# A partition of raw keys and values holds two neighbouring tokens, and the gathers and the mask follow

## The chip, the core and the metric

The kernel runs on one core of one Trainium2 chip. The metric is the device time of one execution in microseconds (us), of which several are taken; lower is better. Engines are named as in the profile: PE (TensorE matmuls) and PEld (its weight loads), DVE (VectorE), ACT (ScalarE), POOL (GpSimd) and SP (SyncE, which here only issues DMAs).

## What is computed

Block-sparse attention followed by a two-layer feed-forward network. There are 4 batches, 8 heads, 768 tokens and a head dimension of 64; blocks have 32 tokens, so there are 24 of them.

```python
batch, n_heads, seq, head_dim = (4, 8, 768, 64)
block = 32
rand_blocks = np.random.randint(0, n_blocks, size=(n_blocks, 3))
...
scores = scale * np.matmul(q, k.transpose(0, 1, 3, 2))
mask = np.abs(blk_i - blk_j) <= window
mask = mask | (blk_i == 0) | (blk_j == 0) | (blk_i == n_blocks - 1) | (blk_j == n_blocks - 1)
for qb in range(n_blocks):
    for kb in sampled_blocks[qb]:
        mask[qb * block:(qb + 1) * block, kb * block:(kb + 1) * block] = True
scores = np.where(mask, scores, -1000000000.0)
attn = np.exp(scores - np.max(scores, axis=-1, keepdims=True))
attn = attn / (np.sum(attn, axis=-1, keepdims=True) + 1e-09)
x = np.matmul(attn, v)          # then (B*S, H*D) = (3072, 512)
...
h = x @ w_in                    # 512 x 2048
out = np.maximum(0.01 * h, h) @ w_out
```

A query block sees its neighbours, the first and the last block, and 3 sampled blocks. The first and the last query block see every key.

## The kernel before

**Tiling.** Two query blocks (64 queries) make a tile T; there are 12 in a batch. T = 0 is the first and the last block together, which see all 768 keys. The others see 384 keys (`KEYS`, 12 slots of 32): a window of 128 tokens from (T-1)*64 on, two end blocks in the last two slots, and in slots 4 to 9 the 3 sampled blocks of each of the two query blocks. A unit is one T and one pair of heads (`hp`), a step of the main loop is one unit, and four tiles T make an item, whose feed-forward part follows later. Every number is carried as two fp16 halves, high and low.

**Keys.** `load_k` (L487) loads a head's 768 x 64 fp32 keys with one DMA: token 128*c + p goes to partition p, chunk c, so each DMA has 768 runs of 256 bytes (192 KB). `prep_k` (L496) takes the sum of squares on ACT, scales, splits into halves and sends them through one DMA transpose into `kt` [128, head, token]. `gather_k` (L587) builds `kg` [128, head, 384] for a tile T: one DVE copy for the window (L593, 8 heads x 128 tokens), one for the two end blocks (L596, done once a batch for each of two buffers), and six POOL copies for the sampled blocks (L602), each at a token offset read from `offs`. It ends with `em` (L607), where POOL spreads the mask of the 12 slots over 32 keys each. `em` is added to the scores (L666).

**Values.** `load_v` (L431) loads the same way. `prep_v` (L437) scales, splits, and writes the halves of a head pair to a DRAM tensor `scr` [768 tokens, 8 heads x 128 fp16], 2 KB a token, with one DMA (L464). `gather_v` (L616) fetches the 384 rows of a tile: one straight DMA for the window (L621), one for each end block (L625, once a batch for each of two buffers), and two indirect DMAs from POOL for the sampled rows (L628), whose row numbers `rows` are made in `build_masks`. The first tile T = 0 reads values from `v16s` in SBUF, in the order of the load.

**Masks.** `build_masks` (L225) makes `offs`, `rows` (block number * 32 or'ed with the lane of the partition) and `mask` [128, 11, 12] fp32: zero, or a large negative number where a slot is not to be counted.

**Order.** The main loop writes the order of work by hand, by a string of letters for each step; side work (loads, `prep_k`, `prep_v`, `prep_q`, weights) is spread between steps as generators. K loads of batch 0 come first of all, then constants, Q, V; K of the next batch follows from step 26 on (for batch 0) or 6 on, V of the next batch from step 28 on. All DMAs except the indirect ones are issued by SP in one queue, the loads, the transposes of `kt`, `qs` and `pt` (L704, probabilities), the `vg` gathers and the outputs. In the first 200 us the feed-forward weights are also loaded (64-bit numbers, decoded with integer operations on DVE, L326 to L330) and split into halves.

```python
t = pa.tile([P, 2, NC, D], F32, tag="rk", ...)
nc.sync.dma_start(out=t[:, h], in_=k[b, 2 * hp + h].rearrange("(c p) d -> p c d", p=P))
...
nc.vector.tensor_copy(out=kg[:, :, :P], in_=kt[:, :, t0:t0 + P])
...
nc.sync.dma_start(out=vg[:, 0, :], in_=scr[b][t0:t0 + P, :])
```

Of the kernel before, what the change touches and what calls it, by code (L numbers as in the profile page):

```python
# [12 lines left out]
BF16 = mybir.dt.bfloat16  # L13
F32 = mybir.dt.float32
I32 = mybir.dt.int32
# [4 lines left out]
P = 128  # L20
BLOCK = 32
WINDOW = 1
NEG = -(2.0 ** 120)
# [42 lines left out]
def tile_block_sparse_attention_ffn(  # L66
# [142 lines left out]
    lane = cst.tile([P, 1], I32, name="lane")  # L209
    mask = cst.tile([P, NT - 1, SLOTS], F32, name="mask")  # L210

# [12 lines left out]

    def build_masks():  # L225
        nc.vector.tensor_scalar(
            out=offs, in0=row.rearrange("p (a b) -> p a b", b=2)[:, :, 0], scalar1=5, scalar2=None,
            op0=ALU.logical_shift_left)
        nc.gpsimd.iota(lane, pattern=[[0, 1]], base=0, channel_multiplier=1)
        nc.vector.tensor_scalar(out=lane, in0=lane, scalar1=BLOCK - 1, scalar2=None, op0=ALU.bitwise_and)  # L230
        flat_rows = rows.rearrange("p c t -> p (c t)")
# [21 lines left out]
        for a in range(2):  # L253
# [5 lines left out]
        nc.vector.tensor_scalar(  # L259
            out=mask[:, :, 4:10], in0=pm.rearrange("p t a r -> p t (a r)"), scalar1=-1.0, scalar2=-NEG,  # L260
            op0=ALU.add, op1=ALU.mult)
        nc.vector.memset(mask[:, :, :4], 0.0)
        nc.vector.memset(mask[:, :, 10:], 0.0)
        for hh in range(2):
            a, b = (slice(D * hh + BLOCK * i, D * hh + BLOCK * (i + 1)) for i in range(2))
            nc.vector.memset(mask[a, :, 3:4], NEG)
            nc.vector.memset(mask[b, :, 0:1], NEG)
            nc.vector.memset(mask[a, 0:1, 10:11], NEG)
            nc.vector.memset(mask[b, NT - 2:NT - 1, 11:12], NEG)

# [158 lines left out]
    vscale, vraw, v16s, scr, vg = {}, {}, {}, {}, {}  # L429

    def load_v(b, hp):  # L431
        t = pa.tile([P, NC, 2, D], F32, tag="v", name=f"v_{b}_{hp}", bufs=5)
        for h in range(2):
            nc.sync.dma_start(out=t[:, :, h, :], in_=v[b, 2 * hp + h].rearrange("(c p) d -> p c d", p=P))
        vraw[b, hp] = t

    def prep_v(b):  # L437
# [14 lines left out]
        for hp in range(NP):  # L452
            raw = vraw.pop((b, hp))
# [13 lines left out]
            yield 1.2  # L467
# [19 lines left out]
    def load_k(b, hp):  # L487
        if b == 0:
            t = early_k[:, hp * S:(hp + 1) * S].rearrange("p (h c d) -> p h c d", h=2, c=NC)
        else:  # L490
            t = pa.tile([P, 2, NC, D], F32, tag="rk", name=f"rk_{b}_{hp}", bufs=CFG["rk"])
        for h in range(2):
            nc.sync.dma_start(out=t[:, h], in_=k[b, 2 * hp + h].rearrange("(c p) d -> p c d", p=P))
        return t
# [92 lines left out]
    def gather_k(b, T):  # L587
# [4 lines left out]
        t0 = (T - 1) * Q2  # L592
        nc.vector.tensor_copy(out=kg[:, :, :P], in_=kt[:, :, t0:t0 + P])  # L593
        if ends.get(n) != b:
            ends[n] = b
            nc.vector.tensor_copy(  # L596
                out=kg[:, :, KEYS - Q2:].rearrange("p h (n l) -> p h n l", l=BLOCK),
                in_=kt.rearrange("p h (n l) -> p h n l", l=BLOCK)[:, :, 0:NB:NB - 1, :])
        for slot, i in sampled_of(T):
            begin = len(nc.cur_bb.bb.instructions)  # L600
            off = nc.gpsimd.value_load(offs[:1, i:i + 1], min_val=0, max_val=S - BLOCK)
            nc.gpsimd.tensor_copy(  # L602
                out=kg[:, :, slot * BLOCK:(slot + 1) * BLOCK], in_=kt[:, :, bass.ds(off, BLOCK)])
# [3 lines left out]
        nc.gpsimd.tensor_copy(  # L607
            out=em.rearrange("p (n l) -> p n l", l=BLOCK),
            in_=mask[:, T - 1, :].unsqueeze(2).to_broadcast([P, SLOTS, BLOCK]))
        kgs[b, T] = kg, em  # L610
# [5 lines left out]
    def gather_v(b, T):  # L616
# [3 lines left out]
        t0 = (T - 1) * Q2  # L620
        nc.sync.dma_start(out=vg[:, 0, :], in_=scr[b][t0:t0 + P, :])  # L621
        if vends.get(n) != b:
            vends[n] = b
            for i, at in enumerate((0, S - BLOCK)):
                nc.sync.dma_start(  # L625
                    out=vg[Q2 + i * BLOCK:Q2 + (i + 1) * BLOCK, 2, :], in_=scr[b][at:at + BLOCK, :])
        for c, n_ in ((1, P), (2, Q2)):
# [577 lines left out]
```

## Time and profile before

| what | value |
|---|---|
| median of 3 runs | 893.37 us (889.02 to 898.08) |
| the profiled execution | 889.45 us, its span 887.7 us |
| mean granted TensorE clock | 0.948 |
| DMA packets | 328,450 (139.25 MB), 295,453 of them under 512 bytes |
| DMAs from SP | 322,718 packets, 66.8% of 16 engines' span |
| K loads (8 into W, 24 into rk) | 32, 192 KB each |
| V loads | 32, 192 KB each, 4.5 us to landing |
| straight gathers of V | 44 of 256 KB, 3.9 us to landing; 16 of 64 KB, 5.3 us |

The span is what the profile covers; about 2 us of the execution lie around it. In the profile a line such as "L602 POOL COPY kg<-kt" is an instruction of line 602 that writes kg from kt. SPq is SP's issuing queue: the time in its rows is that of issuing, not of the transfer. In the view of a tile or a line, three numbers divided by strokes are the least, the median and the longest duration in ns. The view of waits gives the total in us, how often, and the longest. "W<-in_k_dram" are the K loads of batch 0, which use a part of the weights' tile that is still empty.

### The profile page before, as it was taken

To read this page: it belongs to the slowest core of one execution; us is meant where nothing else is said; L and a number is where in the kernel's file an instruction comes from. 1 tells how busy PE (TensorE), PEld (TensorE's weight loads), DVE (VectorE), ACT (ScalarE), POOL (GpSimd) and SP (SyncE) were. 2 spreads that over 40 slices of the span, in tenths; PEclk is the share of its full clock that TensorE was granted. 3 is DMA by queue.
4 is the path that set the end of the run, shared out by engine and by line. 5 is a ranking of instruction groups with operands and counts; after the bars stand their busy time and mean duration, and the time that the engine had idled before them with its cause. 6 is when DMAs were issued, how large, how long until landed. Compare 5 with 4: busy or idle time off the path is not lost. (4 is left out here: it accounts for less than half of the span.)

```text
span 887.7 us, 19902 instructions
## 1 busy us (share of the span) xinstructions
PE 739.8 (83%) x7020; PEld 488.9 (55%) x7020; DVE 624.9 (70%) x1623; ACT 485.8 (55%) x1063; POOL 432.7 (49%) x558
## 2 busy tenths in 40 slices
PE   0234655877999998888999999999899999999997
PEld 0213433645666665555656565656556666656674
DVE  2799898997977886773857867789657677754121
ACT  3666768665655764562645846556536454543211
POOL 0046767565236465664343475476325565633221
PEclk9999555989999999999999999999999999999999
DMA  6998999967679989893558979768836596654000
GB/s 138 272 298 192 280 208 234 207 146 170 141 165 182 197 156 194 137 212 89 145 97 157 217 145 195 169 136 184 194 59 135 106 183 154 126 100 103 20 7 25
DMA packets 328450, 139.25 MB, mean 157 GB/s; under 512 B 295453, under 2 KB 307742, under 8 KB 328350
## 3 DMA queue, kind: packets, MB, share of 16 engines
q1 hardware_dynamic: 322718, 120.67, 66.8%
q0 software_dynamic: 5632, 17.31, 7.6%
q8 instruction: 55, 0.90, 0.4%
q14 instruction: 45, 0.37, 0.1%
HBM read 65.58 MB, written 12.58 MB: 88 GB/s over the span
## 5 line engine op out<-in xcount | busy, mean ns | idle before, releaser
L792 PE MATMUL o<-W,g 128*128 128x512 f16 x1152 | 276.3, 384 | 7.9 <-DVE g L778 6.0
L765 PE MATMUL h<-x,W 128*128 128x256 f16 x2304 | 275.3, 276 | 2.4 <-DVE wi_tot L140 1.1
L765 PEld LDWEIGHTS <-W 128*128 128x128 f16 x2304 | 224.9, 100 | 51.1 <-issue 12.8
L779 POOL TENSOR_TENSOR g<-ht,g 128x512 f16<-128x512 f32 x96 | 114.8, 1196 | 216.8 <-DVE g L778 169.1
L602 POOL COPY kg<-kt 128x256 f16 x264 | 131.4, 521 | 97.0 <-PE s L659 47.7
L792 PEld LDWEIGHTS <-g 128*128 128x128 f16 x1152 | 107.7, 99 | 128.9 <-issue 14.5
L677 ACT ACTIVATE p<-p,mx 128x384 f32<-128x384 f32 x208 | 125.9, 606 | 93.0 <-DVE mx L666 70.8
L699 DVE SCALAR_TENSOR_TENSOR pp<-p,r,pp 128x384 f16<-128x384 f32 x208 | 147.9, 737 | 40.4 <-ACT pp L695 39.1
L695 ACT ACTIVATE pp<-p,r 128x384 f16<-128x384 f32 x208 | 115.6, 605 | 43.8 <-issue 12.9
L628 POOL DMA_INDIRECT vg<-scr,rows x88 | 95.0, 1080 | 61.0 <-PE av L730 40.9
L774 DVE SCALAR_TENSOR_TENSOR ht<-ht 128x512 f32<-128x512 f32 x96 | 71.1, 741 | 75.3 <-ACT ht L771 74.9
L666 DVE CUSTOM_DVE_ANT_0 p<-s,em,nsc 128x384 f32<-128x384 f32 x176 | 101.9, 611 | 25.5 <-PE s L659 25.2
L730 PE MATMUL av<-pt,vg 128*64 128x128 f16 x2112 | 84.8, 230 | 20.6 <-DMA pt<-pp 15.0
L730 PEld LDWEIGHTS <-vg 128*64 128x64 f16 x2112 | 73.5, 117 | 47.3 <-issue 41.3
L771 ACT ACTIVATE ht<-h,gd 128x512 f32<-128x512 f32 x80 | 54.1, 676 | 78.8 <-PE h L765 43.4
L659 PE MATMUL s<-kg,qs_q 128*64 128x384 f16 x352 | 65.6, 368 | 25.0 <-DVE mx L666 20.2
L659 PEld LDWEIGHTS <-qs_q 128*64 128x64 f16 x416 | 28.4, 116 | 85.1 <-issue 46.1
L659 PE MATMUL s<-kg,qxs_q 128*64 128x384 f16 x352 | 64.3, 360 | 6.3 <-DMA qxs_q<-qs_q 6.3
L778 DVE CAST g<-ht 128x512 f16<-128x512 f32 x96 | 43.9, 457 | 12.4 <-PE o L792 10.3
L748 POOL TENSOR_TENSOR x<-xf,x 128x256 f16<-128x256 f32 x48 | 37.1, 773 | 27.8 <-ACT x L746 27.3
L685 DVE TENSOR_SCALAR sum<-sum 128x2 f32<-128x2 f32 x96 | 30.9, 322 | 22.0 <-ACT p L677 21.3
L534 ACT ACTIVATE qa_q<-rq 128x512 f16<-128x512 f32 x25 | 15.7, 626 | 51.8 <-DMA rq<-in_q_dram 40.3
(129 smaller groups left out, 753.6 us busy)
## 6 DMA issues: line engine op xcount, KB each, us to landing
vg<-scr SPq DMA_DIRECT2D x44, 256.0 KB, 3.9
v<-in_v_dram SPq DMA_DIRECT2D x32, 192.0 KB, 4.5
qxs_q<-qs_q SPq DMA_DIRECT2D x48, 128.0 KB, 3.1
scr<-v SPq DMA_DIRECT2D x16, 384.0 KB, 4.2
W<-in_moe_w_in_dram SPq DMA_DIRECT2D x5, 1024.0 KB, 5.9
rq<-in_q_dram SPq DMA_DIRECT2D x20, 256.0 KB, 5.3
out_dram<-ob SPq DMA_DIRECT2D x20, 256.0 KB, 3.4
rk<-in_k_dram SPq DMA_DIRECT2D x24, 192.0 KB, 4.8
```

Source lines behind the costliest of these rows:

```text
L602: nc.gpsimd.tensor_copy(out=kg[:, :, slot * BLOCK:(slot + 1) * BLOCK], in_=kt[:, :, bass.ds(off, BLOCK)])
L628: nc.gpsimd.indirect_dma_start(out=vg[:n_, c, :], out_offset=None, in_=scr[b][:, :], in_offset=bass.IndirectOffsetOnAxis(ap=rows[:n_, c - ...
L659: nc.tensor.matmul(o, a, k, start=(n == 0), stop=(n == 1)))
L666: nc.vector.tensor_tensor_reduce(out=u.p[i], in0=u.sp[i], in1=kgs[u.b, u.T][1] if u.T else zero.to_broadcast([P, KEYS]), scale=u.nsc, scal ...
L677: nc.scalar.activation(u.p[i], u.p[i], AF.Exp, scale=-1.0, bias=u.mx[:, :1], accum_out=u.pair.sum[:, u.pi, i:i + 1])
L695: nc.scalar.activation(pp[:, 0, :], p, AF.Copy, scale=u.r)
L699: nc.vector.scalar_tensor_tensor(out=pp[:, 1, :], in0=p, scalar=u.r, in1=pp[:, 0, :], op0=ALU.mult, op1=ALU.subtract)
L730: nc.tensor.matmul(o, a, m, start=(c == 0 and l == 0), stop=(c == n - 1 and l == 1)))
L765: nc.tensor.matmul(c.ph[:, i], w, x, start=(d == 0 and m == 0), stop=(d == NP - 1 and m == 2)))
L774: nc.vector.scalar_tensor_tensor(out=c.t, in0=c.t, scalar=0.01, in1=c.t, op0=ALU.mult, op1=ALU.max)
L779: nc.gpsimd.tensor_tensor(out=c.g[:, 1], in0=c.t, in1=c.g[:, 0], op=ALU.subtract)
L792: nc.tensor.matmul(o, a, w, start=(c.first and i == 0 and m == 0), stop=(c.last and i == 1 and m == 2)))
```

## The change

K and V are loaded so that partition p of chunk c holds tokens 256*c + 2*p and 256*c + 2*p + 1, which are adjacent in DRAM. A load then has 384 runs of 512 bytes. In the chunks of 128 the even tokens of 256 come first and the odd ones after, and what follows is brought into that order:

- `kt` keeps its shape; its columns are even tokens, then odd tokens, by 256.
- Each run of tokens in `kg` and `vg` is in that order too: 64 even and 64 odd ones in the window, 16 and 16 in each end block and sampled block. The window copy has 2 x 64 elements for each head and is cut in two where the window crosses from one 256-token chunk into the next; the end blocks are two copies; a sampled block is copied as 2 x 16 elements.
- `scr` still has one row a token, in the order of tokens; each head pair is written by two DMAs, one for the even and one for the odd rows. The straight gathers of V are two DMAs each, every second row.
- `offs` and the lanes of `rows` are worked out for that order, with a few more integer operations.
- `mask` has two entries for each slot (even, odd) in bf16, and `em` spreads each over 16 keys. The window's masked blocks are then columns 3 and 7, or 0 and 4.

```diff
-    mask = cst.tile([P, NT - 1, SLOTS], F32, name="mask")
+    mask = cst.tile([P, NT - 1, 2 * SLOTS], BF16, name="mask")
...
+        at_row = row.rearrange("p (a b) -> p a b", b=2)
         nc.vector.tensor_scalar(
-            out=offs, in0=row.rearrange("p (a b) -> p a b", b=2)[:, :, 0], scalar1=5, scalar2=None,
-            op0=ALU.logical_shift_left)
+            out=offs, in0=at_row[:, :, 0], scalar1=3, scalar2=8,
+            op0=ALU.logical_shift_right, op1=ALU.logical_shift_left)
+        nc.vector.tensor_scalar(
+            out=at_row[:, :, 1], in0=at_row[:, :, 0], scalar1=7, scalar2=4,
+            op0=ALU.bitwise_and, op1=ALU.logical_shift_left)
+        nc.vector.tensor_tensor(out=offs, in0=offs, in1=at_row[:, :, 1], op=ALU.bitwise_or)
...
-        nc.vector.tensor_scalar(out=lane, in0=lane, scalar1=BLOCK - 1, scalar2=None, op0=ALU.bitwise_and)
+        nc.vector.tensor_scalar(
+            out=odd, in0=lane, scalar1=4, scalar2=1, op0=ALU.logical_shift_right, op1=ALU.bitwise_and)
+        nc.vector.tensor_scalar(
+            out=lane, in0=lane, scalar1=HB - 1, scalar2=1, op0=ALU.bitwise_and, op1=ALU.logical_shift_left)
+        nc.vector.tensor_tensor(out=lane, in0=lane, in1=odd, op=ALU.bitwise_or)
...
+    pairs = lambda t: t.rearrange("p (c r) d -> p c (r d)", r=2)
...
-        t = pa.tile([P, NC, 2, D], F32, tag="v", name=f"v_{b}_{hp}", bufs=5)
+        t = pa.tile([P, 2, NC, D], F32, tag="v", name=f"v_{b}_{hp}", bufs=5)
         for h in range(2):
-            nc.sync.dma_start(out=t[:, :, h, :], in_=v[b, 2 * hp + h].rearrange("(c p) d -> p c d", p=P))
+            nc.sync.dma_start(out=pairs(t[:, h]), in_=v[b, 2 * hp + h].rearrange("(c p r) d -> p c (r d)", p=P, r=2))
...
-            nc.sync.dma_start(
-                out=scr[b].rearrange("(c p) (g x) -> p g c x", p=P, g=NP)[:, hp],
-                in_=v16.rearrange("p c x d -> p c (x d)"))
+            for r in range(2):
+                nc.sync.dma_start(
+                    out=scr[b].rearrange("(c p r) (g x) -> p r g c x", p=P, r=2, g=NP)[:, r, hp],
+                    in_=v16[:, r::2].rearrange("p c x d -> p c (x d)"))
...
-            nc.sync.dma_start(out=t[:, h], in_=k[b, 2 * hp + h].rearrange("(c p) d -> p c d", p=P))
+            nc.sync.dma_start(out=pairs(t[:, h]), in_=k[b, 2 * hp + h].rearrange("(c p r) d -> p c (r d)", p=P, r=2))
...
-        nc.vector.tensor_copy(out=kg[:, :, :P], in_=kt[:, :, t0:t0 + P])
+        ktv = kt.rearrange("p h (c r t) -> p h c r t", r=2, t=P)
+        win = kg[:, :, :P].rearrange("p h (r j) -> p h r j", r=2)
+        c0, a0 = t0 // (2 * P), t0 % (2 * P) // 2
+        n0 = min(Q2, P - a0)
+        nc.vector.tensor_copy(out=win[:, :, :, :n0], in_=ktv[:, :, c0, :, a0:a0 + n0])
+        if n0 < Q2:
+            nc.vector.tensor_copy(out=win[:, :, :, n0:], in_=ktv[:, :, c0 + 1, :, :Q2 - n0])
...
-            nc.vector.tensor_copy(
-                out=kg[:, :, KEYS - Q2:].rearrange("p h (n l) -> p h n l", l=BLOCK),
-                in_=kt.rearrange("p h (n l) -> p h n l", l=BLOCK)[:, :, 0:NB:NB - 1, :])
+            for i, (c, at) in enumerate(((0, 0), (NC // 2 - 1, P - HB))):
+                nc.vector.tensor_copy(
+                    out=kg[:, :, KEYS - Q2 + i * BLOCK:KEYS - Q2 + (i + 1) * BLOCK].rearrange(
+                        "p h (r j) -> p h r j", r=2),
+                    in_=ktv[:, :, c, :, at:at + HB])
...
+            first = kt[:, :, bass.ds(off, HB)]
+            src = bass.AP(first.tensor, first.offset, [*first.ap[:-1], [P, 2], first.ap[-1]],
+                          runtime_checks=first.runtime_checks, dep_tracking_offset=first.dep_tracking_offset)
             nc.gpsimd.tensor_copy(
-                out=kg[:, :, slot * BLOCK:(slot + 1) * BLOCK], in_=kt[:, :, bass.ds(off, BLOCK)])
+                out=kg[:, :, slot * BLOCK:(slot + 1) * BLOCK].rearrange("p h (r j) -> p h r j", r=2), in_=src)
...
-            out=em.rearrange("p (n l) -> p n l", l=BLOCK),
-            in_=mask[:, T - 1, :].unsqueeze(2).to_broadcast([P, SLOTS, BLOCK]))
+            out=em.rearrange("p (n l) -> p n l", l=HB),
+            in_=mask[:, T - 1, :].unsqueeze(2).to_broadcast([P, 2 * SLOTS, HB]))
...
-        nc.sync.dma_start(out=vg[:, 0, :], in_=scr[b][t0:t0 + P, :])
+        for r in range(2):
+            nc.sync.dma_start(out=vg[r * Q2:(r + 1) * Q2, 0, :], in_=scr[b][t0 + r:t0 + P:2, :])
...
-                nc.sync.dma_start(
-                    out=vg[Q2 + i * BLOCK:Q2 + (i + 1) * BLOCK, 2, :], in_=scr[b][at:at + BLOCK, :])
+                for r in range(2):
+                    nc.sync.dma_start(
+                        out=vg[Q2 + i * BLOCK + r * HB:Q2 + i * BLOCK + (r + 1) * HB, 2, :],
+                        in_=scr[b][at + r:at + BLOCK:2, :])
```

In the diff `HB` is 16, `P` 128, `Q2` 64, `NC` 6 and `BLOCK` 32.

More of the change, by code (lines that the diff above doesn't have):

```diff
@@ L21 @@
 BLOCK = 32
+HB = BLOCK // 2
 WINDOW = 1
@@ L225, in build_masks @@
     def build_masks():
+        at_row = row.rearrange("p (a b) -> p a b", b=2)
         nc.vector.tensor_scalar(
-            out=offs, in0=row.rearrange("p (a b) -> p a b", b=2)[:, :, 0], scalar1=5, scalar2=None,
-            op0=ALU.logical_shift_left)
-        nc.gpsimd.iota(lane, pattern=[[0, 1]], base=0, channel_multiplier=1)
-        nc.vector.tensor_scalar(out=lane, in0=lane, scalar1=BLOCK - 1, scalar2=None, op0=ALU.bitwise_and)
+            out=offs, in0=at_row[:, :, 0], scalar1=3, scalar2=8,
[4 more added lines that the diff above has]
+        nc.vector.tensor_tensor(out=offs, in0=offs, in1=at_row[:, :, 1], op=ALU.bitwise_or)
+        nc.gpsimd.iota(lane, pattern=[[0, 1]], base=0, channel_multiplier=1)
+        odd = cst.tile([P, 1], I32, name="odd")
+        nc.vector.tensor_scalar(
[3 more added lines that the diff above has]
+        nc.vector.tensor_tensor(out=lane, in0=lane, in1=odd, op=ALU.bitwise_or)
         flat_rows = rows.rearrange("p c t -> p (c t)")
@@ L259, in build_masks @@
         nc.vector.tensor_scalar(
[L260 to L263, printed above, removed]
+            out=mask[:, :, 8:20].rearrange("p t (n i) -> p t n i", i=2),
+            in0=pm.rearrange("p t a r -> p t (a r)").unsqueeze(3).to_broadcast([P, NT - 1, 2 * NR, 2]),
+            scalar1=-1.0, scalar2=-NEG, op0=ALU.add, op1=ALU.mult)
+        nc.vector.memset(mask[:, :, :8], 0.0)
+        nc.vector.memset(mask[:, :, 20:], 0.0)
         for hh in range(2):
             a, b = (slice(D * hh + BLOCK * i, D * hh + BLOCK * (i + 1)) for i in range(2))
[L266 to L269, printed above, removed]
+            nc.vector.memset(mask[a, :, 3:8:4], NEG)
+            nc.vector.memset(mask[b, :, 0:8:4], NEG)
+            nc.vector.memset(mask[a, 0:1, 20:22], NEG)
+            nc.vector.memset(mask[b, NT - 2:NT - 1, 22:], NEG)
     WI = 512
@@ L452, in prep_v @@
         for hp in range(NP):
-            raw = vraw.pop((b, hp))
+            raw = vraw.pop((b, hp)).rearrange("p h c d -> p c h d")
             if hp:
@@ L592, in gather_k @@
         t0 = (T - 1) * Q2
[L593 removed]
+        ktv = kt.rearrange("p h (c r t) -> p h c r t", r=2, t=P)
[5 more added lines that the diff above has]
+            nc.vector.tensor_copy(out=win[:, :, :, n0:], in_=ktv[:, :, c0 + 1, :, :Q2 - n0])
         if ends.get(n) != b:
             ends[n] = b
[L596 to L598 removed]
+            for i, (c, at) in enumerate(((0, 0), (NC // 2 - 1, P - HB))):
[3 more added lines that the diff above has]
+                    in_=ktv[:, :, c, :, at:at + HB])
         for slot, i in sampled_of(T):
             begin = len(nc.cur_bb.bb.instructions)
[L601 removed]
+            off = nc.gpsimd.value_load(offs[:1, i:i + 1], min_val=0, max_val=S - P - HB)
+            first = kt[:, :, bass.ds(off, HB)]
+            src = bass.AP(first.tensor, first.offset, [*first.ap[:-1], [P, 2], first.ap[-1]],
+                          runtime_checks=first.runtime_checks, dep_tracking_offset=first.dep_tracking_offset)
             nc.gpsimd.tensor_copy(
[L603 removed]
+                out=kg[:, :, slot * BLOCK:(slot + 1) * BLOCK].rearrange("p h (r j) -> p h r j", r=2), in_=src)
             in_order("k", begin)
```

## Prediction

> **What bounds the kernel now.** I read the page's table of busy time and its 40 slices first, to see which engine fills which stage.
>
> ```profile
> span 887.7 us, 19902 instructions
> ...
> PE 739.8 (83%) x7020; PEld 488.9 (55%) x7020; DVE 624.9 (70%) x1623; ACT 485.8 (55%) x1063; POOL 432.7 (49%) x558
> ...
> PE   0234655877999998888999999999899999999997
> ...
> DVE  2799898997977886773857867789657677754121
> ```
>
> The reader is to see two stages. Up to about 200 us (nine slices of 22.2 us) PE is half empty and DVE is nearly full; after that PE is full. The view by windows puts numbers on it (its columns are the stretch, its length, busy time of PE, PEld, DVE, ACT, POOL, the granted clock, the DMA share and GB/s).
>
> ```profile
> core 0: us, PE busy (x) PEld busy (x) DVE busy (x) ACT busy (x) POOL busy (x), PEclk, DMA share, GB/s
> 0.00:200.00 200.00, 97.44 (x920) 68.25 (x921) 165.23 (x423) 129.66 (x251) 102.02 (x120) 0.81 0.94 219
> 16.00:22.00 6.00, 0.00 (x0) 0.00 (x0) 0.00 (x0) 0.00 (x0) 0.00 (x0) 1.00 0.17 14
> 30.00:40.00 10.00, 2.90 (x17) 1.91 (x16) 7.27 (x34) 8.71 (x18) 0.00 (x0) 1.00 1.02 308
> 40.00:50.00 10.00, 3.05 (x18) 1.96 (x19) 9.90 (x18) 5.57 (x7) 0.00 (x0) 1.00 1.19 226
> 220.00:887.00 667.00, 626.79 (x5917) 409.45 (x5915) 444.71 (x1155) 345.84 (x792) 320.11 (x427) 0.99 0.69 138
> 5.70:9.50 3.80, 1.17 (x4) 1.00 (x4) 1.05 (x8) 2.90 (x6) 0.00 (x0) 1.00 1.30 227
> 10.00:14.00 4.00, 0.00 (x0) 0.00 (x0) 1.64 (x4) 2.85 (x7) 0.00 (x0) 1.00 1.03 302
> 37.00:41.00 4.00, 1.46 (x10) 1.20 (x10) 2.69 (x8) 3.27 (x5) 0.00 (x0) 1.00 1.03 405
> 430.00:430.60 0.60, 0.60 (x5) 0.29 (x3) 0.57 (x2) 0.60 (x2) 0.00 (x0) 1.00 0.96 292
> ```
>
> From 220 us on PE is busy 626.8 of 667 us: only 40 us are left there. In the first 200 us DVE is busy 165.2 and DMA 0.94 of its time; from 40 us DVE has no gap (9.90 of 10). So what decides the length of the first stage is when DVE's saturated stretch can begin (DMA decides that), and how much work DVE then has. The third view, the timeline of SP's queue, shows what stands ahead of that:
>
> ```profile
> 3.78 4.16 SPq L493 DMA_DIRECT2D W<-in_k_dram  x6
> ...
> 11.24 4.78 SPq L221 DMA_DIRECT2D rows<-in_sampled_blocks_dram  x6
> 16.11 4.36 SPq L523 DMA_TRANSPOSE kt<-W  x1
> ...
> 26.44 5.57 SPq L434 DMA_DIRECT2D v<-in_v_dram  x6
> ...
> 33.90 8.62 SPq L493 DMA_DIRECT2D rk<-in_k_dram  x4
> 42.62 5.87 SPq L523 DMA_TRANSPOSE kt<-W  x3
> ```
>
> K loads fill the DMA engines to 9.5 us, the first weight load follows (302 GB/s to 14 us), and then 16 to 22 us shows only the crawl of the `rows` loads (14 GB/s) with every engine idle: they began when the weights had ended. Everything up to here is a chain of transfers; the next stretch, V loads, three weight loads and four K loads of batch 1, is one too (DMA share 1.02 and 1.19), until kt of head pairs 1 to 3 is transposed.
>
> **The change part by part.**
>
> *Longer runs.* Each of the 32 K and 32 V loads moves 192 KB (196,608 bytes) in 768 runs of 256 bytes; after the change in 384 of 512. The row 5.70:9.50 is K loads almost alone: 227 GB/s, so 0.87 us a load. For 512-byte runs the nearest row is 430.00:430.60, writes of `scr`: 292 GB/s, so 0.67 us. That saves 0.19 us a load, 12.4 us of DMA time in all. The lower end is nothing (a store is not a load); the upper end is the 405 GB/s of the weights' 4 KB runs: 0.49 us, a saving of 0.38. I take 0.19, since that row has the same run length. On the path lie batch 0's eight K loads (8 x 0.19 = 1.5 us, ahead of weights, `rows` and the first transpose) and its eight V loads, ahead of the weights that DVE decodes from 40 us: 1.5 us. The four of batch 1 (0.8 us) hold up the last three transposes, but at that time DVE is full, so they count nothing. Sum: -3.0 us. If DVE's stretch were held by something else, all of it would be hidden.
>
> The remaining 44 loads save 8.4 us of the DMA time after 40 us. After 220 us that engine-time could only shorten the waits of PE on DMA:
>
> ```profile
> PE s L659 <- DVE mx L666: 8.1, 6, 1.9
> PE av L730 <- DMA pt<-pp: 7.5, 4, 2.9
> PE s L659 <- DMA qxs_q<-qs_q: 6.7, 7, 1.7
> PE s L659 <- DMA qs_q<-qa_q: 5.7, 2, 3.2
> ```
>
> Those three DMA waits are 19.9 us together; 8.4 us of 667 x 0.69 = 460 us of DMA time is 1.8%, so -0.4 us.
>
> *More DMAs.* Each straight gather of V becomes two of 64 rows (44 to 88), the end blocks 16 to 32, the writes of `scr` 16 to 32: 76 more issues on SP.
>
> ```profile
> L621 SPq DMA_DIRECT2D vg<-scr x44: 325/408/3042, 75.8 to 808.9; - x44
> ...
> L625 SPq DMA_DIRECT2D vg<-scr x16: 377/415/953, 76.4 to 642.4; - x16
> ```
>
> At the median 0.41 us that is 31 us of SP. The second of each pair waits for nothing new (the first has waited for the same buffer); behind it stand the transposes of `pt`, for which PE waits 4 times after 220 us, and the q transposes. Cover is the lag between a transpose and its use; without it each issue costs up to 0.41 us at a place where PE waits (13 such waits in the rows above: 5.3 us, the upper end; the lower end is zero). I take one in the first stage and one later: +0.8 us.
>
> *DVE.* The window copy keeps its 1,024 elements but is two copies where the window crosses a 256-token chunk (T = 4 and 8, 8 times in all), and the end blocks are two copies instead of one (8 times). The view of the tile kg in the first 200 us (least, median and longest time in ns):
>
> ```profile
> L602 POOL COPY kg<-kt x64: 386/402/1457, 51.1 to 199.9; 128x256 f16 x64
> L593 DVE COPY kg<-kt x11: 400/552/1273, 52.2 to 198.8; 128x1024 f16<-128x1024 f16 x11
> L596 DVE COPY kg<-kt x2: 277/280/283, 52.5 to 53.3; 128x512 f16<-128x512 f16 x2
> ```
>
> L596 already copies in runs of 32 elements, and from 512 to 1,024 elements the least time grows by 123 ns, so the fixed part is about 150 ns: shorter runs cost nothing, each extra copy 0.15 us. Before 200 us that is 4 copies, +0.6 us on a full DVE. The four more integer operations in build_masks fall into DVE's idle 16 to 22 us, the mask twice as wide is one small operation at 28 us, with the POOL copies that need it 20 us later: zero, covered by those gaps, and under 1 us if they close.
>
> *POOL.* The 264 sampled copies keep their 256 elements, in 16 runs of 16 instead of 8 of 32; em keeps 384, in 24 runs of 16 (its source is now bf16).
>
> ```profile
> L607 POOL CAST em<-mask x10: 497/502/1365, 29.0 to 190.1; 128x384 bf16<-128x384 f32 x10
> ```
> ```profile
> L779 POOL TENSOR_TENSOR g<-ht,g x96: 1141/1156/1999, 168.6 to 878.5; 128x512 f16<-128x512 f32 x96
> ```
> ```profile
> L748 POOL TENSOR_TENSOR x<-xf,x x48: 657/672/1380, 102.4 to 840.2; 128x256 f16<-128x256 f32 x48
> ```
> ```profile
> L387 POOL TENSOR_TENSOR W<-W x12: 2114/2135/3111, 61.0 to 173.1; 128x1024 f16<-128x1024 f32 x12
> ```
>
> The first is em in the same 200 us, the others are the lines of three POOL subtractions. From 386 ns (8 runs, 256 elements) and 497 (12 runs, 384) a run of 32 costs 28 ns. If all of that were the run and none the elements, 8 more runs would add 222 ns and 12 more 333: the upper end. The lower end is zero, and the nearest row speaks for it: L748 walks 4 runs of 64, and lies on the line through the unbroken L779 and L387 (1.90 ns an element, 168 fixed: 654 for 256, measured 657). I take zero.
>
> *Sum.* -3.0 - 0.4 + 0.8 + 0.6 = -2.0 us. Against the profiled execution (889.45 us, of which the span is 887.7) that gives 887.5; this execution is 3.9 us below the median of the runs shown, so as a median 893.4 - 2.0 = 891.4 us.
>
> **The rivals.**
>
> *A, the loads gain far more.* If 512-byte runs went at the rate of 4 KB runs (405 GB/s) and every load before 200 us counted (20 to 43 us, and the eight V loads of batch 1, issued from step 28 on), 28 x 0.38 = 10.6 us would go; less 1.0 for the DVE copies and one issue: 883.8 us. For it: DMA share 0.94 over 200 us. Against it: 292 GB/s for 512 bytes, and DVE's 9.90 of 10. The Trainium skill, DMA: Bandwidth & Descriptors, section Specifications, speaks for this case: it puts the least transfer for line rate at 512 bytes. This trace does not agree as far as it shows: 512-byte stores stay at 292 GB/s where 4 KB loads reach 405.
>
> *B, POOL's short runs.* At the upper end the 64 sampled copies and 10 of em before 200 us cost 64 x 0.222 + 10 x 0.333 = 17.5 us, and where DVE is full a copy that DVE then waits for costs one for one: 893.4 - 2.0 + 17.5 = 908.9 us. It eats the gain from 31 ns a copy, and is slower by 1% from 62% of the bound (138 ns a copy). For it: L593 has a least time of 400 ns and a longest of 1,273, so DVE copies do get held up. Against: L748. The Trainium skill, SBUF — State Buffer, section SBUF: two separate sides, says that DVE and GpSimd take a shared pair of ports as an exclusive lock for a whole instruction; the spread of L593 agrees.
>
> *C, the gain is hidden.* DVE's stretch is held by the weights' arrival and its own work, not by K and V: then only the costs stay, +0.6 + 0.4: 894.4 us. For it: DVE is full from 40 us; against: from 16 to 22 us and for 2.7 us between 30 and 40 it stands idle while transfers run.
>
> **How the numbers follow.** The forecast has 0.45, with its own range 889 to 895 (from 3.0 + 0.8 + 0.4 us of gain and no cost, to the costs of 1.4 alone); A 0.20, B 0.15, C 0.20. The range 883 to 902 takes in A, C and 60% of B's bound. A difference under 1% cannot be told from no change here (the three runs lie 1% apart). Faster by over 1% is A: 0.20. Slower by over 1% is B beyond 138 ns, 0.12; the rest, 0.68, is within 1%.
>
> **What would show it.** The window in which the K loads stand alone should reach about 290 GB/s, and the first kt transpose be issued some 1.5 us before 16.11, the three later ones 3 to 4 us before 42.62. L602's least time should stay at 386 ns (from 420 on B is at work) and the copies L593 at 400 for 1,024 elements. PE's busy time after 220 us should not change. The prediction is wrong if kt comes no earlier, if DVE's busy time before 200 us grows by over 2 us, or if SP's extra issues appear as waits of PE on pt.

## The result, and the profile after

| | median | of runs | ratio to before |
|---|---|---|---|
| kernel before | 894.70 us (889.02 to 901.92) | 20 | |
| changed kernel | 900.15 us (895.40 to 907.86) | 20 | 1.0068, 95% interval 1.0043 to 1.0093 |

The change makes the kernel 0.7% (6 us) slower. The forecast was 891.4 us, 2 us faster. The time lies within the range and within 1% of before, but on the other side of no change, and clear of it. The profiled execution took 897.59 us, of which the span is 895.6. Ratios here and below leave out runs that took over 1.5% more than the fastest of the same kernel, and need not be the quotient of the medians beside them.

First the page's busy time, then the view by windows (columns as before: stretch, length, busy time of PE, PEld, DVE, ACT and POOL, granted clock, DMA share, GB/s).

```profile
span 895.6 us, 20016 instructions
...
PE 744.0 (83%) x7020; PEld 487.7 (54%) x7020; DVE 630.3 (70%) x1643; ACT 486.7 (54%) x1063; POOL 425.5 (48%) x558
```
```profile
0.00:200.00 200.00, 95.57 (x896) 63.89 (x897) 166.63 (x419) 127.14 (x245) 92.58 (x115) 0.81 0.90 213
5.20:8.50 3.30, 1.17 (x4) 1.00 (x4) 0.84 (x7) 2.51 (x6) 0.00 (x0) 1.00 0.96 266
16.00:22.00 6.00, 0.00 (x0) 0.00 (x0) 2.49 (x9) 0.00 (x0) 0.00 (x0) 1.00 0.19 12
40.00:50.00 10.00, 3.21 (x20) 1.99 (x18) 9.39 (x29) 5.32 (x10) 5.91 (x12) 1.00 1.01 328
220.00:887.00 667.00, 628.84 (x5919) 410.50 (x5917) 447.57 (x1171) 347.67 (x796) 321.02 (x430) 0.98 0.72 139
```

The engines' work is nearly the same: PE 744 us against 740, DVE 630 against 625, POOL 425 against 433. In the first 200 us, though, PE has done fewer matmuls (896 against 920) with DVE as full as before. The K loads reach 266 GB/s in place of 227, and the crawl from 16 to 22 us is still there. The timeline of SP's queue shows what became of the earlier start:

```profile
3.65 3.27 SPq L508 DMA_DIRECT2D W<-in_k_dram  x6
...
10.35 6.34 SPq L222 DMA_DIRECT2D rows<-in_sampled_blocks_dram  x6
16.79 4.27 SPq L538 DMA_TRANSPOSE kt<-W  x1
...
30.59 8.88 SPq L538 DMA_TRANSPOSE kt<-W  x3
...
53.48 3.66 SPq L508 DMA_DIRECT2D rk<-in_k_dram  x3
```

Two things stand here. The loads ahead of `rows` are issued 0.9 us sooner, but the six `rows` loads now take 6.34 us to issue instead of 4.78, and the first kt transpose comes at 16.79 instead of 16.11. And the queue has another order: the three later kt transposes stand ahead of the K loads of batch 1 (30.59 against 53.48), where before they stood behind them. Nobody wrote that order by hand. The program writes its instructions down in one sequence, and a planner then places them on each engine by times that it estimates itself; it planned the changed program anew.

The view of kg in the first 200 us, and the two straight gathers from the view of vg:

```profile
L628 POOL COPY kg<-kt x60: 386/401/882, 41.9 to 195.0; 128x256 f16 x60
L612 DVE COPY kg<-kt x10: 288/452/642, 42.5 to 191.6; 128x1024 f16<-128x1024 f16 x8, 128x512 f16<-128x512 f16 x2
L618 DVE COPY kg<-kt x4: 213/410/424, 43.0 to 44.6; 128x256 f16<-128x256 f16 x4
```
```profile
L648 SPq DMA_DIRECT2D vg<-scr x88: 444/588/1586, 74.9 to 817.2; - x88
L653 SPq DMA_DIRECT2D vg<-scr x32: 406/418/2159, 76.2 to 650.2; - x32
```

POOL's copies take 386 ns at the least and 401 at the median, as before: short runs cost POOL nothing. But a gather of 64 rows takes 0.588 us to issue, longer than one of 128 rows did (0.408).

### The profile page after: what moved, and what is told of

It reads as the page before. It is cut to its first block, busy times and chain, and to the rows that moved or that the text cites. A ratio compares the mean times of both kernels' runs of the same rounds, so it can differ in the third digit from the quotient of the medians.

```text
span 895.6 us, 20016 instructions
## 1 busy us (share of the span) xinstructions
PE 744.0 (83%) x7020; PEld 487.7 (54%) x7020; DVE 630.3 (70%) x1643; ACT 486.7 (54%) x1063; POOL 425.5 (48%) x558
## 5 line engine op out<-in xcount | busy, mean ns | idle before, releaser
L794 PE MATMUL h<-x,W 128*128 128x256 f16 x2304 | 278.3, 278 | 5.3 <-DVE q_tot L141 2.7
L794 PEld LDWEIGHTS <-W 128*128 128x128 f16 x2304 | 225.5, 100 | 56.5 <-issue 18.2
L728 DVE SCALAR_TENSOR_TENSOR pp<-p,r,pp 128x384 f16<-128x384 f32 x208 | 151.2, 751 | 48.3 <-ACT pp L724 44.4
L628 POOL COPY kg<-kt 128x256 f16 x264 | 124.4, 493 | 82.7 <-PE s L688 37.7
L688 PE MATMUL s<-kg,qs_q 128*64 128x384 f16 x352 | 63.8, 360 | 39.0 <-DVE mx L695 35.3
L759 PEld LDWEIGHTS <-vg 128*64 128x64 f16 x2112 | 71.3, 116 | 41.7 <-issue 35.0
L714 DVE TENSOR_SCALAR sum<-sum 128x2 f32<-128x2 f32 x96 | 37.0, 386 | 19.8 <-ACT p L706 19.2
L777 POOL TENSOR_TENSOR x<-xf,x 128x256 f16<-128x256 f32 x48 | 37.3, 777 | 21.2 <-ACT x L775 20.3
```

The costliest lines, as they stand in the source:

```text
L628: nc.gpsimd.tensor_copy(out=kg[:, :, slot * BLOCK:(slot + 1) * BLOCK].rearrange("p h (r j) -> p h r j", r=2), in_=src)
L688: nc.tensor.matmul(o, a, k, start=(n == 0), stop=(n == 1)))
L728: nc.vector.scalar_tensor_tensor(out=pp[:, 1, :], in0=p, scalar=u.r, in1=pp[:, 0, :], op0=ALU.mult, op1=ALU.subtract)
L759: nc.tensor.matmul(o, a, m, start=(c == 0 and l == 0), stop=(c == n - 1 and l == 1)))
L794: nc.tensor.matmul(c.ph[:, i], w, x, start=(d == 0 and m == 0), stop=(d == NP - 1 and m == 2)))
```

## Experiments

The runs e1 to e4, e5 to e8, e9 to e11, e12 to e14, e15 and e16, e17 and e18 each shared a chip with runs of the kernel before; each ratio is to those runs. The same kernel came out 0.2 to 0.4% apart on two chips (below), so differences within a group weigh most. The quotient of the medians would be up to 0.4% away from the ratio (0.998 for e3, 1.015 for e7): a difference that small is weak evidence by itself.

### Is it the order or the contents?

To part the two, the order in which one kernel's engines run can be written into another. Instructions of the two programs are matched by line and operation; then each is tied to the one ahead of it on its engine, without a wait, so that the planner has no choice left (`ORDER` holds one list for each engine). Additional instructions stand right behind their partners. Tying them costs nothing that shows: e11 and e16 below, held to the order of the kernel before, come to 0.9992 and 1.0011.

```diff
+    order = json.loads(zlib.decompress(base64.b85decode(ORDER)))
+    traced = [i for i in nc.cur_bb.bb.instructions if not type(i).__name__.startswith("BassTilePool")]
+    for steps in order.values():
+        at, before = 0, None
+        for d in steps:
+            at += d
+            if before is not None:
+                tc.add_manual_dep(traced[at], before.name, mybir.DependencyInfo(
+                    mybir.DependencyClass.NoSync, mybir.DependencyReason.DATA), reason="pin")
+            before = traced[at]
```

The same match says how far the planner went: of the instructions that both kernels have, the number outside the longest common order is 262 of 1,407 on DVE, 490 of 6,966 on PE and 68 of 427 on SP. For the loads alone (e4) it is much the same: 302 on DVE, 559 on PE.

**e1, the whole change in the order of before.**

> All of the change, but on every engine the instructions stand in the order of the kernel before (each additional DMA or copy right behind its partner). If the order that the planner made of the changed kernel costs the time (theory O), this is at or below before: ratio 0.996 to 1.001 (the forecast's own sum says 0.998). If what the instructions themselves do costs it (theory C: more DMAs on SP, DVE held up by POOL), it stays at the changed kernel's ratio, 1.004 to 1.009.

**e2, the kernel before in the order of the changed one.**

> The kernel before, instruction for instruction, but on every engine in the order that the planner gave the changed kernel. Theory O: as slow as the changed kernel, ratio 1.004 to 1.010. Theory C: as before, 0.998 to 1.002.

**e3, the longer runs of the loads alone, in the order of before.**

```diff
-            nc.sync.dma_start(out=t[:, h], in_=k[b, 2 * hp + h].rearrange("(c p) d -> p c d", p=P))
+            nc.sync.dma_start(out=pairs(t[:, h]), in_=k[b, 2 * hp + h].rearrange("(c p r) d -> p c (r d)", p=P, r=2))
```

> Only the K and V loads have 512-byte runs (tokens are then in another order than the gathers and the mask take them, which are as before); every engine in the order of the kernel before. By the forecast's term for the loads (3.4 us of gain): ratio 0.996, between 0.994 and 0.998. If the loads' gain is hidden: 0.999 to 1.001.

**e4, the same in the planner's own order.**

> The same kernel as the one before it, but in the order that the planner makes of it (302 of 1,407 DVE and 559 of 6,966 PE instructions out of their place). Theory O: it differs from that kernel by an amount that nothing in the loads explains, ratio 1.002 to 1.010 to the kernel before, or below 0.994. Theory C: equal to that kernel within 0.2%.

| group 1 | median | ratio to before | 95% interval |
|---|---|---|---|
| e1 whole change, old order | 897.96 us | 1.0023 | 0.9996 to 1.0049 |
| e2 before, new order | 906.94 us | 1.0104 | 1.0054 to 1.0155 |
| e3 loads alone, old order | 894.45 us | 1.0001 | 0.9968 to 1.0034 |
| e4 loads alone, own order | 903.56 us | 1.0086 | 1.0051 to 1.0121 |

The order alone costs 1.0% (e2) with not one instruction changed, and 0.85% between e3 and e4. The loads alone, in the old order, show no gain; the interval leaves room for one of 0.3%. What the planner does differently shows in the view by windows of two lines alone, from 60 to 100 us: the last step of decoding a piece of a weight (first row of each pair) and the row maximum of the attention scores (second row). The columns are the stretch, its length, DVE's busy time with these instructions and their count, clock, DMA share, GB/s. The kernel before, e3, the changed kernel, e4:

```profile
60.00:100.00 40.00, 5.06 (x4) 0.81 0.92 223
60.00:100.00 40.00, 7.10 (x24) 0.81 0.92 223
```
```profile
60.00:100.00 40.00, 5.06 (x4) 0.90 0.81 196
60.00:100.00 40.00, 7.13 (x24) 0.90 0.81 196
```
```profile
60.00:100.00 40.00, 5.98 (x5) 0.80 0.82 185
60.00:100.00 40.00, 4.86 (x17) 0.80 0.82 185
```
```profile
60.00:100.00 40.00, 7.34 (x6) 0.79 0.96 225
60.00:100.00 40.00, 3.62 (x12) 0.79 0.96 225
```

The second row counts two instructions for each score tile, the maximum and the reading of its result. So in the old order DVE handles 12 score tiles in this stretch and decodes 4 pieces; in the new orders it decodes 5 or 6 and handles 8 to 9, or 6 (e2: 5 and 7). PE waits for the maximum. The view of PE's waits before 220 us (total in us, how often, the longest), the kernel before and the changed one:

```profile
PE s L659 <- DVE mx L666: 20.0, 13, 5.3
```
```profile
PE s L688 <- DVE mx L695: 37.3, 14, 7.6
```

This wait is 19 to 26 us in the kernels that are held to the old order throughout, 37.3 in the changed kernel and 39.5 in e2. For all the decoding ahead the weights are no sooner complete: the last decoding step ends at 194.0 us before, at 193.6 after. But the 48th score tile ends at 235.2 us instead of 227.5, and the last one is as late (815.2 against 807.4).

e4 does not fit this account. It decodes ahead most of all, is done with it at 178.1 us, has its 48th tile at 225.0, waits 24.5 us for the maximum, and is still 0.86% slower. That the order costs is shown for e4 too; by what path is open there.

**e5 and e6: where in the kernel the order costs.** The lists of e1 and of the changed kernel are joined at one point.

> The changed kernel. Up to the last weight decode and about the 50th attention unit (some 230 us) its engines follow the order of the kernel before, from there on the order that the planner gave to the changed kernel. Out of place against before: 44 instructions of DVE (262 in the changed kernel), 192 of PE (490), 23 of SP (68). Theory S (the order costs its time in the first stage, where weights are decoded ahead of attention units): the ratio to before is that of all in the old order, 1.000 to 1.004, and the 24th weight decode ends at about 105 us, unit 32 at about 150 us. Rival T (the order costs its time later, where PE is full): the ratio is that of the changed kernel, 1.006 to 1.010.

> The converse: the changed kernel in its own order up to the same point, and in the order of the kernel before from there on. Theory S: ratio 1.006 to 1.010, the 24th weight decode ends at about 90 us, unit 32 at about 156 us, and the 5 to 8 us by which the units lag then do not come back. Rival T: 1.000 to 1.004.

**e7: DVE's order alone.**

> The changed kernel with only DVE held to the order of the kernel before; the planner places the other engines round it. If it is DVE's order in the first stage that costs (theory S), the ratio is 1.000 to 1.004 and the 24th weight decode ends near 105 us. If it is the order of PE, SP or POOL, the ratio stays at 1.006 or more, although DVE decodes no earlier than before.

| group 2 | median | ratio | 95% interval |
|---|---|---|---|
| e5 old order to 230 us, own after | 897.22 us | 1.0026 | 0.9985 to 1.0066 |
| e6 own order to 230 us, old after | 905.68 us | 1.0146 | 1.0112 to 1.0181 |
| e7 only DVE in the old order | 907.98 us | 1.0182 | 1.0143 to 1.0221 |
| e8 before, with two DMAs (below) | 900.92 us | 1.0088 | 1.0056 to 1.0120 |

On one chip, the order up to 230 us makes a difference of 1.2% (e5 and e6); with the old order there, the rest may be as the planner likes (1.0026). In e6 PE waits 36.6 us for the maximum before 220 us, in e5 25.5. The profiled execution of e6 was its fastest (896.19 us), so it shows only a part of the loss. e6 is dearer than the changed kernel itself, and e7 dearer than any: a part of one plan beside a part of another can be worse than either, so e7 doesn't say whose order it is that costs.

### The two DMAs

**e8: the kernel before, with nothing added but the cut of gathers and writes.**

```diff
-        nc.sync.dma_start(out=vg[:, 0, :], in_=scr[b][t0:t0 + P, :])
+        for r in range(2):
+            nc.sync.dma_start(out=vg[r * Q2:(r + 1) * Q2, 0, :], in_=scr[b][t0 + r * Q2:t0 + (r + 1) * Q2, :])
```

> The kernel before, its loads, tokens and order unchanged, but each straight gather of V and each write of scr cut into two DMAs (halves of adjacent rows), each extra one behind its partner: 76 more issues on SP, nothing else. If the extra issues are what is left of the loss when the whole change runs in the old order (measured ratio 1.0023), the ratio is 1.002 to 1.005, and waits of PE on kt or qxs_q grow by some 3 us between 220 and 300 us. The prediction's term of 2 issues (0.8 us) gives 1.001. If SP's time is covered, 1.000.

The ratio is 1.0088, above the 1.0023 of the whole change in the same order (e1, on another chip). **e12** is meant to part issuing from moving data:

```diff
         nc.sync.dma_start(out=vg[:, 0, :], in_=scr[b][t0:t0 + P, :])
+        nc.sync.dma_start(out=spare, in_=scr[b][t0:t0 + Q2, :16])
```

> The kernel before in its own order, with 60 more DMAs on SP, one right behind each straight gather of V and each end block, as many as the change adds there; each moves 2 KB or 0.5 KB in pieces of 32 bytes to a tile that nobody reads. If the cut of the gathers costs by SP's issue time (0.4 to 0.6 us each, 25 to 35 us in all), the ratio is 1.004 to 1.009. If it costs by the smaller DMAs themselves (data in two landings), 1.000 to 1.002.

It came to 900.48 us, ratio 1.0056 (1.0027 to 1.0086). 60 DMAs with hardly any data behind them cost about half a per cent, so more than the halved transfers is at work. The view of the tile spare (least, median and longest issue in ns):

```profile
L711 SPq DMA_DIRECT2D spare<-scr x44: 456/471/1527, 78.8 to 823.8; - x44
L717 SPq DMA_DIRECT2D spare<-scr x16: 302/308/403, 86.8 to 664.4; - x16
```

That is 25.7 us at the medians, for some 5 us of time. But issuing isn't all that e12 adds. Its small DMAs all write one tile, and the view of SP's waits shows the queue standing still for an earlier one of them, 23.6 us in all:

```profile
SPq L717 <- DMA spare<-scr: 23.6, 14, 6.8
```

So e12 shows that DMAs which move next to nothing hold up the queue; how much of that is the issuing itself, it doesn't show. One place where the cut gathers make the queue late can be seen in SP's timeline, where batch 1 begins. The kernel before and then e1:

```profile
263.98 0.35 SPq L621 DMA_DIRECT2D vg<-scr  x1
264.43 0.38 SPq L625 DMA_DIRECT2D vg<-scr  x1
...
266.88 0.95 SPq L625 DMA_DIRECT2D vg<-scr  x1
...
275.70 0.79 SPq L621 DMA_DIRECT2D vg<-scr  x1
276.58 0.85 SPq L625 DMA_DIRECT2D vg<-scr  x2
278.50 1.23 SPq L546 DMA_TRANSPOSE qs_q<-qa_q  x1
...
283.81 0.47 SPq L548 DMA_DIRECT2D qxs_q<-qs_q  x1
```
```profile
263.17 1.11 SPq L736 DMA_DIRECT2D vg<-scr  x2
264.38 1.00 SPq L741 DMA_DIRECT2D vg<-scr  x2
...
266.98 1.82 SPq L741 DMA_DIRECT2D vg<-scr  x2
...
276.97 1.52 SPq L736 DMA_DIRECT2D vg<-scr  x2
278.58 1.93 SPq L741 DMA_DIRECT2D vg<-scr  x4
281.54 2.75 SPq L649 DMA_TRANSPOSE qs_q<-qa_q  x1
...
289.96 0.48 SPq L651 DMA_DIRECT2D qxs_q<-qs_q  x1
```

The gathers take 3.32 us of SP in the one and 7.38 in the other. e1 is 0.8 us ahead at their start; its q transpose comes 3.0 us later and qxs, which the scores of the next unit need, 6.2 us later. The table follows this stretch by the end of the 48th, 64th and 96th of the 208 score tiles, read from the timeline of each profiled execution. Its last column is the sum of PE's waits for DMAs from 220 to 887 us.

| old order | 48th | 64th | between | 96th | PE's waits for DMAs |
|---|---|---|---|---|---|
| before | 227.5 | 291.7 | 64.2 us | 394.1 | 19.9 us |
| e3 loads alone | 227.5 | 292.3 | 64.8 us | 391.0 | 16.8 us |
| e16 before, outputs from ACT (below) | 228.5 | 294.0 | 65.5 us | 392.4 | 17.2 us |
| e11 before, `rows` late (below) | 225.5 | 292.6 | 67.1 us | 392.7 | 20.3 us |
| e12 60 small DMAs | 234.7 | 300.4 | 65.7 us | 402.3 | 24.2 us |
| e8 cut gathers alone | 232.6 | 301.0 | 68.4 us | 399.8 | 24.0 us |
| e1, e17 whole change | 226.8, 228.9 | 295.9, 296.8 | 69.1, 67.9 us | 393.2, 394.8 | 24.8, 25.5 us |
| e13, e18 all but the loads | 229.2, 231.7 | 298.1, 299.8 | 68.9, 68.1 us | 397.7, 398.5 | 23.2, 25.0 us |

Between the 48th and the 64th tile the kernels with cut gathers lose 4 to 5 us (e11, with whole ones, 3). By the 96th they have this back: against the kernel before, each stands within 2 us of where it stood at the 48th. So batch 1 shows how the queue gets late, and not where the time at the end is lost. The last column tells the kernels apart: 17 to 20 us with whole gathers, 23 to 25 with additional DMAs (e14 and e15, 23.7 and 24.0), in the mean 18.6 against 24.3. These are waits for the transfers of kt, qs, qxs and pt; a wait for the gathered rows themselves stands in e17 alone (1.5 us). That speaks for the queue, and against data that comes in two landings. In which stretch the loss that lasts arises stays open: from the 96th tile to the last the kernels with cut gathers fall behind by another 6.5 to 8.7 us, but so does e11 with whole ones (8.5) in the one execution that was profiled.

**e9: one DMA for each gather, in the same broken row order.**

```diff
-        for r in range(2):
-            nc.sync.dma_start(out=vg[r * Q2:(r + 1) * Q2, 0, :], in_=scr[b][t0 + r:t0 + P:2, :])
+        nc.sync.dma_start(
+            out=vg[:, 0, :], in_=scr[b][t0:t0 + P, :].rearrange("(j r) x -> r j x", r=2))
```

> The changed kernel in the order of the kernel before, with one DMA in place of two for each straight gather of V and each end block: the same rows, fetched by one access pattern that names the even rows first, then the odd ones. 60 fewer issues on SP than in the changed kernel; the 16 extra writes of scr stay. Theory P (extra issues cost some 0.9% and the longer runs of the loads give some 0.65%, and the two add up): of the 49 us of extra SP time 38 are of vg, so the ratio falls from 1.0023 to 0.994 to 0.997. Rival Q (the loads' gain only fills what the extra issues take; without them there is nothing for it to shorten, as in the kernel with the loads alone, 1.0001): 0.999 to 1.001. Rival R (not SP's issuing but the broken row order of the gathers costs): 1.002 or more, and the single DMA takes as long to issue as two.

999.40 us, ratio 1.1181 (1.1128 to 1.1234): all three theories miss by far. Issuing one such DMA takes 557 ns at the median, about as long as one half gather; it is the transfer that is slow. A window over a straight gather in e9, then one in the kernel before, each with little else on the DMA engines:

```profile
76.70:82.80 6.10, 4.68 (x67) 3.64 (x68) 6.10 (x15) 6.10 (x9) 5.22 (x7) 1.00 0.13 48
```
```profile
786.30:787.80 1.50, 1.50 (x14) 0.71 (x13) 1.03 (x4) 0.88 (x3) 0.51 (x1) 1.00 0.64 175
```

A DMA share of 0.13 is 2.1 of 16 engines at 48 GB/s, where the plain gather has 0.64 and 175 GB/s. Everything behind it in the queue waits. The Trainium skill, DMA: Bandwidth & Descriptors, section Why a DMA increments its semaphore by 16 and not by 1, gives the reason: the number of engines is the largest up to 16 that divides the slowest dimension of both patterns, here the 2 of even and odd. The trace agrees, with 2.1 busy.

### Do the loads gain anything?

**e13: the whole change without the longer runs**, in the old order (in the changed kernel, K and V loaded as the first line of e3's diff has it).

> The changed kernel in the order of the kernel before, with K and V loaded as before, in runs of 256 bytes (so tokens stand in an order that the gathers do not expect; the work is the same). Against the whole change in the old order (1.0023) only the length of the runs differs. If the loads give what the extra issues make room for: 1.006 to 1.011, as in the kernel with the two DMAs alone (1.0088). If the loads give nothing here either, 1.000 to 1.005, and the two DMAs alone cost for another reason.

It came to 901.80 us, ratio 1.0081 (1.0047 to 1.0116), which with e1's 1.0023 looked like a gain of 0.6%. But those are two chips, so both ran again on one.

> The whole change in the order of the kernel before, once more, beside the next kernel on one chip. If the first reading holds, 1.000 to 1.005. If the loads' longer runs give nothing, the same ratio as the next kernel, 1.005 to 1.010.

> The same kernel with K and V loaded in runs of 256 bytes (tokens then stand in an order that the gathers do not expect). If the loads gain some 0.6% here: 1.005 to 1.011, and 0.004 to 0.008 above the kernel beside it. If not, within 0.002 of it.

| one chip | median | ratio | 95% interval |
|---|---|---|---|
| e17 whole change, old order | 899.37 us | 1.0044 | 1.0016 to 1.0072 |
| e18 all but the loads, old order | 900.17 us | 1.0037 | 1.0009 to 1.0065 |

There is no difference that shows, and e18 is 0.4% below what e13 had been. In the traces the loads do bring the first stage forward: the last decoding step ends at 192.9 us in e17 and at 198.3 in e18 (193.2 and 196.3 in e1 and e13). Of those 3 to 5 us, 2 are left when the last score tile ends (816.7 and 818.4, 815.2 and 817.5). So the gain of the loads beside the cut gathers lies between nothing and some 0.5%; it isn't settled further.

### Does the crawl of rows hide it?

**e11: the kernel before with the `rows` loads behind the kt transposes**, and e10, e9 with the same move.

> The kernel before with only the rows loads and their operation moved in the same way, every other instruction in its old order. If the crawl of rows sets the start of the first stage, 3 to 8 us less than before (ratio 0.991 to 0.997), and the first kt transpose at 11 to 12 us instead of 16.1. If not, 1.000; if the crawl only moves to a worse place (weights and qxs_q behind it), 1.002 to 1.006.

> The same with the six rows loads moved on SP's queue from ahead of the first kt transpose to behind the transposes of head pairs 1 to 3 and the second q, and DVE's operation on rows moved to about 64 us. If the crawl of rows (16 to 22 us) hides the loads' gain, the first kt transpose is issued at 10.5 to 12 us instead of 16.8, DVE's weight decoding starts some 5 us earlier, and the time falls by 3 to 8 us against the same kernel with rows ahead (ratio 0.4 to 0.9% lower); the gain over the kernel before with rows moved in the same way is then 2 to 3 us more than without the move. If the first stage is held by DVE's or the DMA engines' own work, neither ratio moves by over 0.2%.

```profile
11.10 1.68 SPq L611 DMA_TRANSPOSE kt<-W  x1
...
34.93 5.77 SPq L611 DMA_TRANSPOSE kt<-W  x3
...
42.47 3.14 SPq L309 DMA_DIRECT2D rows<-in_sampled_blocks_dram  x6
```
```profile
40.00:50.00 10.00, 3.08 (x16) 1.28 (x17) 7.96 (x24) 8.40 (x13) 4.79 (x11) 1.00 0.52 77
```

The first stage does start sooner in e11: the first transpose by 5.0 us, the next three by 7.7. The time doesn't change by more than the interval: 893.25 us, ratio 0.9992 (0.9954 to 1.0030). The crawl now stands at 42 us, where DVE loses 2 of 10 us (77 GB/s). Decoding ends 1.7 us sooner (192.3), and at the 64th score tile nothing is left (292.6 against 291.7). e10 is as slow as e9 (1.1185), and its gathers hide anything else.

**e14: the whole change with `rows` issued by ACT** (`nc.scalar.dma_start`).

> The whole change in the order of the kernel before, with the six rows loads issued by ACT at its start, where it stands idle, instead of by SP at 10 us. If the crawl of rows on SP's queue hides the loads' gain: the first kt transpose at about 10.5 us, the first weight decode at about 12 us, and the ratio 0.003 to 0.008 below the 1.0023 of the same kernel without this. If the first stage takes the same time whatever its start (as when rows were moved on SP's queue: 0.9992), the ratio stays within 0.002 of 1.0023, and a start 5 us earlier is gone again by 200 us.

899.91 us, 1.0054 (1.0021 to 1.0087): no gain. The six K loads that took SP 3.27 us took 6.75, and the first kt transpose came at 18.4 us: the small pieces hold up whatever runs beside them.

### Relieving SP

**e15 and e16: outputs issued by ACT**, in the whole change and in the kernel before, both in the old order.

> The whole change in the order of the kernel before, with the 32 output DMAs issued by ACT in place of SP, each at the place in ACT's order that it had in the order of all engines. SP is relieved of some 17 us, nearly all after 240 us. If each us of SP after 240 us costs as it did when issues were added (about 5 us of time for 29 us of SP), the ratio falls by 0.003 from 1.0023, to about 0.999. If SP has slack there and only issues at certain places count, it stays within 0.001 of 1.0023. If ACT is held up by the outputs, it rises above 1.004.

> The kernel before with the same 32 DMAs issued by ACT, all else in its order. If SP's time bounds the kernel before as well: ratio 0.996 to 0.998. If only added issues cost, since the order was made for those that it has: 1.000. If ACT is held up: above 1.002.

902.38 us, 1.0099 (1.0059 to 1.0140), and 895.39 us, 1.0011 (0.9978 to 1.0044). Taking 17 us off SP gives nothing that shows. SP's total is not a bound in the kernel before. That only what stands ahead of a transfer that is waited for counts would fit this; no run shows it by itself. Why e15 came out dearer than e1 stays open: its profiled execution is 3 us behind e1's at 196 us (end of decoding), where the two still run the same instructions, so a part of it at least isn't the outputs.

## Why the prediction was wrong

*The order.* The step that failed first is one that the prediction didn't have: its sum takes every instruction of both kernels to stand in the same place on its engine. In the measured kernel 262 of 1,407 DVE instructions and 68 of 427 of SP stand elsewhere. That costs 0.85 to 1.2% between kernels of one chip that differ in order (e3 and e4, before and e2, e5 and e6), and about 0.35% in the changed kernel: 1.0068, against 1.0033 for e1 and e17 together, a difference of 0.0035 +- 0.0031, and one between chips. None of the rivals has it.

*More DMAs.* "I take one in the first stage and one later: +0.8 us". Measured alone, 1.0037 to 1.0088 (e18, e13, e8), 3.3 to 7.9 us. Two sizes were off. The halves don't take the 0.408 us of a whole gather but 0.588, so SP's gathers went from 36.2 to 74 us in all and its writes of `scr` from 10 to 20. And the cover was counted on PE's waits in the trace of before, 13 places at one issue each; but where batch 1 begins, five groups of gathers stand ahead of one q transpose within 18 us, and the 4 us that they take more all arrive there. One place can be charged several issues, though that one is made good by the 96th tile. In the traces in the old order PE's waits for DMAs after 220 us are some 6 us longer with the additional DMAs, above the 5.3 us that were the upper end; the times alone don't decide whether the upper end was too low.

*Longer runs.* "-3.0 us". The rate was near what was taken (266 GB/s in the changed kernel and 251 in e3 against 292 taken, before 227). What failed is the premise that the length of the first stage is decided by when DVE's stretch can begin. The first transpose came no sooner, since the `rows` loads took up what was won. The three later ones did, by 4.7 us in e3 (issued at 37.95 us), more than was forecast, and the last decoding step still ended at 194.3 us against 194.0. In e11 a start 5 to 8 us sooner is worth 1.7 us at 192 us and nothing that shows at the end. Rival C named that case for the loads, at 0.20, and e3 bears it out (1.0001; the forecast's gain would be 0.9962, just outside its interval). The Trainium skill, DMA: Bandwidth & Descriptors, section Specifications, puts line rate from 512 bytes on; now that loads show it, 251 to 266 GB/s against 405 for runs of 4 KB is not line rate here either.

*DMA waits of PE, -0.4 us.* After 220 us they came to 19.9 us before. In e1, which has the same order, they are 24.8 us:

```profile
PE s L776 <- DMA qxs_q<-qs_q: 9.8, 7, 2.1
...
PE av L847 <- DMA pt<-pp: 6.2, 2, 3.3
PE s L776 <- DMA qs_q<-qa_q: 5.4, 3, 3.2
PE s L776 <- DMA kt<-k_k: 3.4, 1, 3.4
```

The one on kt had no row before. The prediction looked for SP's extra issues in the waits on pt; these did not grow, those on kt and qxs did. With whole gathers these sums already differ by 3.5 us between executions (16.8 in e3 to 20.3 in e11), so a gain of 0.4 us could not be seen.

*DVE, +0.6 us.* Right in kind: busy time before 200 us grew by 1.4 us, below the 2 us named, and the copies of 1,024 elements cost no more for their shorter runs (549 ns in the mean, 589 before).

*POOL, zero.* Right: 386 ns, as before. Rival B, dearest of the three, is out, though the time came out on its side. Rival A is out too: e3 gains nothing.

Put together, with the kernels in the old order weighted by their intervals: cut gathers and writes +0.65% (e8, e13, e18), the longer runs bring that to +0.33% (e1, e17; the step least sure, as e17 and e18 show), and the planner's new order to +0.68%. Taken in another sequence the steps have other sizes: in the new order the kernel before is at 1.0104 (e2) and the changed one at 1.0068, and PE's waits for DMAs after 220 us are no longer with cut gathers (15.6 us) than with whole ones (16.4 in e2). So the costs don't simply add up, and the measured kernel, by its trace, pays in its first stage (7.7 us late at the 48th score tile, 7.8 at the last). That the time came within 1% of the forecast is luck: a gain that isn't there and two costs that weren't seen are all small. No version that was tried is clearly faster than the kernel before.

## What to carry over

Where a planner orders the instructions by its own estimates, a change of many of them is two changes, the instructions and a new order; pin the order of one kernel in the other before a difference under 1% is put down to the instructions. A DMA that is cut in two makes the queue late for the transfers behind it, by several issues at once if they stand ahead of the same one; but a lag at one place may be made good later, so follow it to the end before it is counted. And a head start in a first stage is worth only what is left of it at the end of the next: move the start by itself and look, before it is counted.

## What the runs showed of the hardware

- A gather of 64 rows of 2 KB takes SP longer to issue (0.588 us) than one of 128 (0.408), and 64 pieces of 32 bytes still 0.471.
- One DMA whose outer dimension is 2 ran on about 2 of the 16 DMA engines: 48 GB/s in place of 175, and the kernel 11.8% slower.
- Six loads in pieces of 4 bytes hold their neighbours wherever they stand: 12 to 14 GB/s from 16 to 22 us, 77 GB/s from 40 to 50 us (e11), and K loads that issue in 6.75 us instead of 3.27 (e14).
- Two executions of the same instructions can be 3 us apart after 196 us (e1 and e15), and the same kernel 0.2 to 0.4% apart against its neighbour on two chips (e1 and e17, e13 and e18).
